# The seam between two networks: last operands in smaller steps, first copies ahead of weight casts

## The chip, the cores and the metric

One core of one Trainium2 chip. The metric is the device time of one execution in microseconds (us); before the change the median of three runs is 704.36 us. Engines are named as in the profile: PE (TensorE), DVE (VectorE), ACT (ScalarE), POOL (GpSimd), SP (SyncE, which only issues DMAs here).

## The reference, cut to what matters

```python
def _moe_ref(x, w_in, w_out):            # x: 1152 x 512, from attention; w_in 512 x 2048
    h = x @ w_in
    return np.maximum(0.01 * h, h) @ w_out            # this result is called y below

def _moe2_ref(x, domain_probs, w1, w2):  # x: y; 4 experts, w1 512 x 1024, w2 1024 x 512
    p = domain_probs / (domain_probs.sum(-1, keepdims=True) + 1e-09)
    out = 0
    for e in range(4):
        out += p[:, e:e + 1] * (np.maximum(x @ w1[e], 0.0) @ w2[e])
```

Causal attention with a decay bias (2 batches, 8 heads, 576 positions, 64 wide) comes first and gives x. The change touches the end of the first network and the start of the second.

## The kernel before, in words

All operands of matmuls are split into a rounded part and a remainder ("hi" and "lo", fp32r): a product of two tensors is three matmuls (hi by hi, lo by hi, hi by lo). ACT makes hi with a cast, DVE or POOL makes lo with a subtract.

The 1152 tokens are in two sets, set 0 of 512 and set 1 of 640. Feature-major matrices are multiplied as 2 x 2 blocks with seven block products in place of eight (`block_products`): each of the seven is 2 pairs x 3 = 6 matmuls, and four PSUM banks collect them. The order matters here: product 0 goes into bank 0; ACT copies bank 0 into `u2` (tile `tmp`); products 1, 2 and 3 go into the other banks while DVE adds up `u2` and `u4`; then three more products go *onto* banks 0, 2 and 3, which have to have been read by then. One side of a product needs prepared combinations of the four blocks of the activations (`paired_steps`, tile `t`, seven operands with hi and lo), the other side those of the weights (`seven_steps`, `seven_in_place`, `eight`, made by ACT casts and POOL).

The first network on set 1 (`mlps(phases[1])`) ends with `down1`: its results y (tile `y`, one per set, each 4 feature blocks d) are summed in SBUF by DVE, block by block in the order d = 0, 2, 1, 3, and for set 1 in two halves of 320 columns. `paired_steps(1, ...)` makes from y of set 1 the operands of the second network: first for k = 0 (feature blocks 0 and 2), then for k = 1 (blocks 1 and 3). It is a generator; the loop at its call lets it go on one step now and then between the steps of `mlps`, and empties it at the end.

The second network (`second`) runs eight blocks of half an expert each. A block has four groups of up products, here called one to four: `up_part` with pair 0 and 1 of the weights on set 0 (columns of 256: groups one and two), then pair 0 and 1 on set 1 (columns of 320: groups three and four). Groups one and two are evicted by `sevens_of`, which makes the seven operands for the down product: ACT and DVE work through the banks, four sums land in a tile `sums` of one buffer, ACT casts them, and POOL subtracts for their lo part. Then come `down2_sevens` (set 0, products of 256 columns) and `down2` (set 1, five tiles of 512 columns). Both need the two down weights of the block, each made by `eight`: a plain split (cast on ACT, subtract on POOL), four in-place combinations on POOL, and a second split. `down2` uses the plain part alone.

Weights come in by `fetch`, which `next_w` calls with a look-ahead of two pieces; raw pieces are loaded by SP into tiles `raw`. At the seam the pools of the first network (`rawp` with four raw tiles, and `ypool` with both y) are closed, and the second network's pools (`rawp2`, `wdown`) are laid over their space.

Up to the line `fixed = False` every instruction is kept in program order (class `InOrder`). After it, the order on each engine is made by the framework's scheduler, from its own model of when each instruction is ready; it places an instruction that is ready early ahead of those before it in the code. `tc.keep_in_program_order(ins)` pins one: it is queued behind the instruction that was traced last on the same engine. The subtracts of `paired_steps` are pinned so already. Each engine then takes its queue strictly in order. Since a helper records every operation, all rows show line 43; tiles tell the operations apart.

Of the kernel before, what the change touches and what calls it, by code (L numbers as in the profile page):

```python
# [9 lines left out]
F32 = mybir.dt.float32  # L10
# [9 lines left out]
def attention_moe_moe2(ctx: ExitStack, tc: tile.TileContext, q, k, v, s, w_in, w_out, probs, w1, w2, out):  # L20
# [7 lines left out]

    fixed = True

    class InOrder:

# [4 lines left out]
        def __getattr__(self, name):  # L39
            call = getattr(self.engine, name)  # L40

            def issue(*args, **kw):
                ins = call(*args, **kw)  # L43
                return tc.keep_in_program_order(ins) if fixed else ins

            return issue

# [17 lines left out]
    P = 128  # L65
    KD = DM // P
# [10 lines left out]
    sizes = (512, 2 * S - 512)  # L77

    const = ctx.enter_context(tc.tile_pool(name="const", bufs=1))
    first = ctx.enter_context(ExitStack())  # L80
    rawp = first.enter_context(tc.tile_pool(name="rawp", bufs=RAW))
    ypool = first.enter_context(tc.tile_pool(name="ypool", bufs=1))
    dram = ctx.enter_context(tc.tile_pool(name="dram", bufs=1, space=bass.MemoryType.DRAM))

    def f32(ap):
        return ap.bitcast(F32)
# [121 lines left out]
    def load_w(src, shape, unit):  # L208

        raw = rawp.tile([P, 1024], F32, tag="raw", name="raw")  # L210
        if unit is None:
            nc.sync.dma_start(raw.rearrange("p (a b) -> p a b", a=shape[0]), src)
        else:
            nc.sync.dma_start(raw, w_f32[unit])
        return raw
# [47 lines left out]
        return w  # L263

    def eight(raw):

        w = wpool.tile([P, 2, 8, 256], F32R, tag="w", name="w")
        b11, b12, b21, b22 = (raw[:, i * 256 : (i + 1) * 256] for i in range(4))

        def split(i):  # L270
            hi, lo = (w[:, l, i : i + 4].rearrange("p s c -> p (s c)") for l in range(2))
            nc.scalar.copy(hi, raw)
            nc.gpsimd.tensor_tensor(lo, raw, f32(hi), ALU.subtract)

        split(0)
        nc.gpsimd.tensor_tensor(b22, b22, b12, ALU.subtract)
        nc.gpsimd.tensor_tensor(b12, b12, b11, ALU.subtract)
        nc.gpsimd.tensor_tensor(b11, b22, b11, ALU.add)
        nc.gpsimd.tensor_tensor(b21, b21, b11, ALU.subtract)
        split(4)  # L280
        return w

    def first_sevens():

# [55 lines left out]
    stream, r64s, raws, kept, ready = [], [], {}, {}, []  # L340
# [3 lines left out]
    def fetch(n):  # L344

        if fixed:
            return
        for i in range(len(ready), min(n, len(stream))):
            if i not in raws:
                raws[i] = load_w(*stream[i][:3])  # L350
        for i in range(len(ready), min(n, len(stream))):
            ready.append(split_w(raws.pop(i), stream[i][1], stream[i][4]))

    used, w7pool = 0, None
# [26 lines left out]
    x_t, y_t, oacc, touched = [], {}, {}, {}  # L381
# [35 lines left out]
    def down1(f, c, h, w):  # L417

        if f == 0:
            y_t[c] = ypool.tile([P, KD, sizes[c]], F32, tag=f"y{c}", name=f"y{c}")  # L420
        for d in (0, 2, 1, 3):
            for lo, hi in halves(c):
                ps = ps_mm.tile([P, 512], F32, tag="mm", name="ps_d")[:, : hi - lo]
                sl, cols = slice(d * P, (d + 1) * P), slice(lo, hi)
                at_h = [at(x, cols) for x in h] if c == 0 else [at(x, j, cols) for x in h for j in range(2)]
                yield from in_steps(ps, [(at(w[i // 2], i % 2, sl), x) for i, x in enumerate(at_h)])
                ya = y_t[c][:, d, cols]
                if f == 0:
                    nc.scalar.copy(ya, ps)
                else:  # L430
                    nc.vector.tensor_tensor(ya, ps, ya, ALU.add)
                yield

    t7 = {}

    def paired_steps(s, of, pool):

        n = half[s]
        t = t7[s] = pool.tile([P, 2, 7, 2, n], F32R, tag=f"t7_{s}", name=f"t7_{s}")
        for k in range(2):  # L440
            b11, b12 = of[:, k, :n], of[:, k, n:]
            b21, b22 = of[:, 2 + k, :n], of[:, 2 + k, n:]
            sums = scratch.tile([P, 4 * 320], F32, tag="scratch", name="sums")[:, : 4 * n].rearrange("p (s t) -> p s t", s=4)
            def subtract(*args):
                tc.keep_in_program_order(nc.vector.tensor_tensor(*args, ALU.subtract))

            subtract(sums[:, 1], b12, b11)
            subtract(sums[:, 2], b22, sums[:, 1])
            yield
            subtract(sums[:, 3], b22, b12)  # L450
            subtract(sums[:, 0], b21, sums[:, 2])
            yield
            for i, j, x in ((0, 2, of[:, k::2, :n]), (2, 3, of[:, 2 + k : 3 + k, n:]), (3, 7, sums)):
                hi, lo = (t[:, l, i:j, k] for l in range(2))
                nc.scalar.copy(hi, x)
                subtract(lo, x, f32(hi))
                yield

    def paired_up(w, s, leaky):

# [45 lines left out]

    def block_products(name, n, operands):

        tmp = scratch.tile([P, 2 * 320], F32, tag="tmp", name="tmp")[:, : 2 * n].rearrange("p (i t) -> p i t", i=2)
        u2, u4 = (tmp[:, i] for i in range(2))  # L510
        bank = [ps_mm.tile([P, 512], F32, tag="mm", name=f"{name}{i}")[:, :n] for i in range(4)]

        def product(to, a, b, onto=False):
            products(bank[to], operands(a, b), onto)

        def add(to, of, x):
            nc.vector.tensor_tensor(to, of, x, ALU.add)

        product(0, 0, 0)
        nc.scalar.copy(u2, bank[0])  # L520
        product(1, 4, 5)
        add(u2, bank[1], u2)
        product(2, 3, 4)
        add(u4, bank[2], u2)
        product(3, 5, 6)
        add(bank[1], bank[3], u4)
        product(0, 1, 1, True)
        product(2, 6, 2, True)
        add(bank[2], bank[2], u2)
        product(3, 2, 3, True)  # L530
        add(bank[3], bank[3], u2)
        return bank
# [42 lines left out]

    def second(blocks):

        w, h = {}, {}

        def up_part(i, pair, s):  # L580
            if (i, pair) not in w:
                (w[i, pair],) = next_w(1)
            h.setdefault(i, ({}, {}))[pair][s] = paired_up(w[i, pair], s, False)

        for pair, s in ((0, 0), (1, 0), (0, 1), (1, 1)):
            up_part(0, pair, s)
        for i, (e, _, _) in enumerate(blocks):
            wd = next_w(2)
            down2_sevens(e, h[i], wd)
            down2(e, h.pop(i), wd)  # L590
            if i + 1 < len(blocks):
                for pair, s in ((0, 0), (1, 0), (0, 1), (1, 1)):
                    up_part(i + 1, pair, s)

    def mlps(blocks):
        hs = {}
        for what, (e, f, c), pair in in_order(blocks):
            h = hs.setdefault(f, [])
            if what == "down":
                yield from down1(f, c, h, next_w(2))  # L600
            elif c == 0 and f == 0:
                if pair == 0:
                    yield from opening(h)
            elif c == 0:
                yield from up1(next_w(1)[0], h)
            else:
                h.append(paired_up(next_w(1)[0], c, True))
                yield
# [387 lines left out]
    hpool = None  # L996
    look = 2
    t7pool = scratch = None
    last_mlp = False
    x_t.extend((None, ypool.tile([P, KD, sizes[1]], F32, tag="y1", name="x1")))  # L1000
    with ExitStack() as phase:
        x_t[0] = phase.enter_context(tc.tile_pool(name="x0pool", bufs=1)).tile([P, 2, KD, sizes[0]], F32R, name="x0")
        wpool = phase.enter_context(tc.tile_pool(name="wpool", bufs=4))
# [7 lines left out]
        with tc.tile_pool(name="early", bufs=1) as early:  # L1011
            ones = pads(early)
            sums = cumulative()
# [3 lines left out]
            for at_ in range(3 * 64):  # L1017
                i = next(side)
# [35 lines left out]
        scratch = phase.enter_context(tc.tile_pool(name="scratch", bufs=2))  # L1054
# [22 lines left out]
    with ExitStack() as phase:  # L1077
        wpool = phase.enter_context(tc.tile_pool(name="wpool", bufs=3))
        hidden_pool(phase, 3)
        scratch = phase.enter_context(tc.tile_pool(name="scratch", bufs=2))  # L1080
        tokens, rest = paired_steps(0, y_t[0], t7early), None
        last = 2 * len(phases[1]) + 32 * (len(phases[1]) - 1) + 16
        for i, _ in enumerate(mlps(phases[1])):
            if i >= 12 and i % 6 == 0:
                next(tokens, None)
            if i >= last:
                rest = rest or paired_steps(1, y_t[1], t7pool)
                if i % 4 == 1 and i < last + 16:
                    next(rest)
        for _ in tokens:  # L1090
            pass
        for _ in rest:
            pass
    first.close()
    last_mlp = True
    rawp = ctx.enter_context(tc.tile_pool(name="rawp2", bufs=2))
# [44 lines left out]
```

## Time and profile before

| | |
|---|---|
| three runs | 703.07, 704.36, 706.07 us |
| the profiled execution | 702.2 us, of which its span 700.4 |
| granted TensorE clock, mean | 0.997 of full speed |
| busy share of the span | PE 97%, PEld 89%, DVE 68%, ACT 50%, POOL 57% |
| stretch of the second network | from about 324 us to the end |

The profile is of one execution. Times in the rows count from the span's start. A timeline merges neighbouring instructions of one kind on one engine into a row: start, duration of the whole, how many; in brackets the idle time of the engine in front of it, and the engine and tile that ended it. PE is the matmul, PEld the weight load beside it. The chain of work goes back from the last instruction, at each step to what released it.

### The profile page before, as it was taken

How to read it: one execution, taken by the hardware profiler on the slowest of the kernel's cores; microseconds unless marked ns; L12 is line 12 of the kernel's file. 1: busy time of each engine (PE TensorE's matmuls, PEld its weight loads, DVE VectorE, ACT ScalarE, POOL GpSimd, SP SyncE). 2: the span in 40 equal slices, each digit the busy share in tenths (PEclk: the TensorE clock that was granted, in tenths of full speed). 3: DMA queues.
4: the chain of work that ended last, by engine and by line, in shares of the span. 5: the costliest groups of instructions: out<-in, count | busy, mean ns of one | idle time of the engine just before them, and what ended most of it. 6: DMA issues, size and time to landing. Idle time of an engine off the chain costs nothing.

```text
span 700.4 us, 12025 instructions
## 1 busy us (share of the span) xinstructions
PE 678.0 (97%) x4496; PEld 623.2 (89%) x4496; DVE 476.2 (68%) x1043; ACT 352.7 (50%) x726; POOL 401.3 (57%) x382
## 2 busy tenths in 40 slices
PE   8899999899989999998999999999999999999998
PEld 7788777778869999998999989989999899998997
DVE  6878899888798558537764747647656476465573
ACT  5768978966655765534533515415244253252520
POOL 6000213222178888952985949949679499496830
PEclk9999999999999999999999999999999999999999
DMA  8886689746632321101120110201101111112003
GB/s 225 202 221 205 189 233 269 214 138 236 225 125 79 120 91 62 61 1 61 41 53 29 61 61 6 88 30 61 61 1 61 61 34 59 31 61 61 1 31 105
DMA packets 42282, 69.15 MB, mean 99 GB/s; under 512 B 5664, under 2 KB 25904, under 8 KB 42224
## 3 DMA queue, kind: packets, MB, share of 16 engines
q1 hardware_dynamic: 32976, 40.30, 19.7%
q0 software_dynamic: 6016, 20.71, 9.5%
q10 hardware_dynamic: 3232, 7.38, 3.2%
q8 instruction: 35, 0.57, 0.4%
q14 instruction: 23, 0.19, 0.1%
HBM read 57.54 MB, written 10.82 MB: 98 GB/s over the span
## 4 chain that ended last, share of the span: by engine, by line
PE 70%; DVE 9%; issue 7%; DMA 6%; ACT 4%; POOL 4%; ACTq 0%; SPq 0%; POOLq 0%; DVEq 0%
PE ps_d L43 35%; PE ps_u L43 32%; DVE raw L43 2%; DMA r<-in_moe_w_out_dram 2%; DVE w L43 2%; PE ps_sc L43 1%; DVE z L43 1%; POOL w L43 1%; PE ps_o L43 1%; DMA vs<-in_v_dram 1%; ACT z L43 1%; PE ps_pt L43 1%; POOL raw L43 1%; DMA ke<-in_k_dram 1%; ACT w L43 1%
## 5 line engine op out<-in xcount | busy, mean ns | idle before, releaser
L43 PE MATMUL ps_u<-t,w 128*128 128x320 f32 (+1 forms) x1680 | 236.2, 299 | 3.0 <-ACT tmp L43 2.0
L43 POOL TENSOR_TENSOR w<-raw,w 128x512 fp32r<-128x512 f32 (+2 forms) x116 | 181.6, 1584 | 95.6 <-ACT w L43 95.5
L43 PEld LDWEIGHTS ps_u<-t,w 128*128 128x128 f32 x1680 | 229.9, 189 | 4.6 <-ACT tmp L43 2.4
L43 PE MATMUL ps_d<-w,ht 128*128 128x256 f32 (+1 forms) x1164 | 195.2, 326 | 0.0
L43 PEld LDWEIGHTS ps_d<-w,ht 128*128 128x128 f32 x1164 | 173.3, 190 | 18.3
L43 ACT CAST w<-raw 128x512 fp32r<-128x512 f32 (+2 forms) x138 | 98.1, 738 | 137.4 <-PE ps_d L43 88.8
L43 ACT ACTIVATE ht<-ps_u 128x320 fp32r<-128x320 f32 (+2 forms) x160 | 68.5, 436 | 93.1 <-DVE ps_u L43 67.0
L43 PE MATMUL ps_d<-ht,w 128*128 128x320 f32 (+1 forms) x576 | 108.7, 339 | 3.2 <-DVE ht L43 3.2
L43 PEld LDWEIGHTS ps_d<-ht,w 128*128 128x128 f32 x576 | 91.3, 188 | 9.6 <-DVE ht L43 3.6
L43 POOL TENSOR_TENSOR raw<-raw 128x256 f32<-128x256 f32 x120 | 86.2, 738 | 2.2
L43 DVE SCALAR_TENSOR_TENSOR oacc<-ps_d,pn,oacc 128x256 f32<-128x256 f32 (+1 forms) x92 | 51.4, 579 | 46.7 <-PE ps_d L43 46.0
L43 DVE TENSOR_TENSOR ps_u<-ps_u,tmp 128x320 f32<-128x320 f32 (+1 forms) x120 | 56.1, 470 | 34.1 <-PE ps_u L43 32.5
L43 DVE TENSOR_TENSOR tmp<-ps_u,tmp 128x320 f32<-128x320 f32 (+1 forms) x80 | 36.7, 462 | 34.6 <-PE ps_u L43 23.4
L43 DVE SCALAR_TENSOR_TENSOR ht<-ps_u,ht 128x320 fp32r<-128x320 f32 (+1 forms) x112 | 49.7, 455 | 14.3 <-ACT ht L43 14.3
L43 POOL DMA_DIRECT2D w_f<-raw x13 | 8.3, 636 | 86.8 <-DVE raw L43 73.3
L43 PE MATMUL ps_u<-x,w 128*128 128x512 f32 x192 | 56.4, 413 | 0.9 <-DVE x L43 0.9
L43 ACT ACTIVATE z<-z,mn 128x256 f32<-128x256 f32 (+4 forms) x72 | 42.5, 590 | 9.4 <-DVE mn L43 8.5
L43 DVE CUSTOM_DVE_ANT_0 z<-ps_sc,mask 128x256 f32<-128x256 f32 (+4 forms) x72 | 35.9, 499 | 10.4 <-PE ps_sc L43 6.7
L43 POOL TENSOR_TENSOR ht<-sums,ht 128x1024 fp32r<-128x1024 f32 x16 | 38.6, 2410 | 6.5 <-ACT ht L43 6.5
L43 ACT COPY pv<-ps_pt 128x512 f32<-128x512 f32 (+3 forms) x80 | 33.0, 422 | 17.8 <-PE ps_pt L43 17.5
L43 DVE TENSOR_TENSOR ht<-ps_u,ht 128x320 fp32r<-128x320 f32 (+1 forms) x48 | 26.5, 555 | 22.0 <-ACT ps_u L43 21.8
L43 PE MATMUL ps_pt<-ident,z 128*128 128x128 f32 x200 | 34.6, 276 | 6.8 <-ACT pv L43 6.0
(97 smaller groups left out, 774.1 us busy)
## 6 DMA issues: line engine op xcount, KB each, us to landing
raw<-in_moe_w_dram SPq DMA_DIRECT2D x32, 512.0 KB
raw<-w_f SPq DMA_DIRECT2D x21, 512.0 KB
w_f<-raw POOLq DMA_DIRECT2D x13, 512.0 KB, 3.5
r<-in_moe_w_out_dram POOLq DMA_DIRECT2D x6, 1024.0 KB, 7.4
r<-in_moe_w_in_dram POOLq DMA_DIRECT2D x5, 1024.0 KB, 7.6
r<-in_moe_w_in_dram ACTq DMA_DIRECT2D x3, 1024.0 KB
kd<-in_k_dram POOLq DMA_DIRECT2D x8, 288.0 KB, 8.1
kr<-in_k_dram SPq DMA_DIRECT2D x8, 288.0 KB
```

The source lines that it names most:

```text
L43: ins = call(*args, **kw)
```

## The change

`InOrder` gets a list `pinned` of engines whose instructions are pinned although `fixed` is false. It is used in three places: for DVE in the last 17 steps of the first network and the rest of `paired_steps`; for ACT's copy of bank 0 in groups one and two of the first block; for ACT in the second part of the first down weight and the whole second one.

`paired_steps` for set 1 is called with `halved`: for k = 1 its operands that are plain blocks of y are split singly as soon as their half of y is summed, and what depends on the last half comes in one step at the end. The steps at which it goes on are others.

`eight` is cut into a plain split and the rest. For the first block the look-ahead is set to nothing; the first down weight is loaded and its plain split traced before group one, its rest and the whole second weight after group two. `ypool` becomes two pools, one for each set's y.

```diff
-                return tc.keep_in_program_order(ins) if fixed else ins
+                return tc.keep_in_program_order(ins) if fixed or self.engine in pinned else ins
...
-    ypool = first.enter_context(tc.tile_pool(name="ypool", bufs=1))
+    ypools = [first.enter_context(tc.tile_pool(name=f"ypool{i}", bufs=1)) for i in range(2)]
...
     def eight(raw):
+        steps = eight_steps(raw)
+        next(steps)
+        return next(steps)
+
+    def eight_steps(raw):
...
         split(0)
+        yield
         nc.gpsimd.tensor_tensor(b22, b22, b12, ALU.subtract)
...
         split(4)
-        return w
+        yield w
...
-    def paired_steps(s, of, pool):
+    def paired_steps(s, of, pool, halved=False):
...
+            if k == 0 and halved:
+                break
+        if halved:
+            b11, b12, b21, b22 = of[:, 1, :n], of[:, 1, n:], of[:, 3, :n], of[:, 3, n:]
+            sums = scratch.tile([P, 4 * 320], F32, tag="scratch", name="sums")[:, : 4 * n].rearrange("p (s t) -> p s t", s=4)
+
+            def split(i, j, x):
+                hi, lo = (t[:, l, i:j, 1] for l in range(2))
+                nc.scalar.copy(hi, x)
+                subtract(lo, x, f32(hi))
+
+            subtract(sums[:, 1], b12, b11)
+            split(0, 1, of[:, 1:2, :n])
+            yield
+            split(1, 2, of[:, 3:4, :n])
+            yield
+            subtract(sums[:, 2], b22, sums[:, 1])
+            subtract(sums[:, 3], b22, b12)
+            subtract(sums[:, 0], b21, sums[:, 2])
+            split(2, 3, of[:, 3:4, n:])
+            split(3, 7, sums)
+            yield
...
+        was, pinned = pinned, (tc.nc.scalar,) if opening_last else pinned
         nc.scalar.copy(u2, bank[0])
+        pinned = was
...
+        look, opening_last = 0, True
+        steps = eight_steps(load_w(*stream[len(ready)][:3]))
+        next(steps)
         for pair, s in ((0, 0), (1, 0), (0, 1), (1, 1)):
             up_part(0, pair, s)
+            if (pair, s) == (1, 0):
+                pinned = (tc.nc.scalar,)
+                ready.append(next(steps))
+                fetch(used + 2)
+                look, pinned, opening_last = 2, (), False
...
         for i, _ in enumerate(mlps(phases[1])):
+            pinned = (tc.nc.vector,) if i + 1 >= last else ()
...
             if i >= last:
-                rest = rest or paired_steps(1, y_t[1], t7pool)
-                if i % 4 == 1 and i < last + 16:
+                rest = rest or paired_steps(1, y_t[1], t7pool, True)
+                if i - last in (1, 3, 5, 7, 9, 10, 13):
                     next(rest)
```

## Rows read from the trace of the kernel before

**Rows 1.** The page, part 1: busy us (share of the span), instructions.

```profile
PE 678.0 (97%) x4496; PEld 623.2 (89%) x4496; DVE 476.2 (68%) x1043; ACT 352.7 (50%) x726; POOL 401.3 (57%) x382
```

**Rows 2.** List of PE's waits: us in total, times, longest.

```profile
PE ps_u L43 <- ACT tmp L43: 2.0, 1, 2.0
...
PE ps_u L43 <- ACT sums L43: 1.0, 1, 1.0
```

**Rows 3.** Timeline of PE, 312 to 346 us: start, duration, [idle before].

```profile
323.94 5.92 PE L43 MATMUL ps_u<-t,w 128*128 128x256 f32 x48
331.84 11.20 PE L43 MATMUL ps_u<-t,w 128*128 128x256 f32 x78 [1.98 <-ACT tmp L43]
344.06 1.15 PE L43 MATMUL ps_u<-t,w 128*128 128x320 f32 x6 [1.02 <-ACT sums L43]
```

**Rows 4.** Chain of work that ended last, from 344 us: start, duration, what.

```profile
345.20 0.72 PE ps_d L43 x6
...
348.56 0.71 PE ps_d L43 x6
349.27 0.88 PE ps_u L43 x6
350.15 1.30 PE ps_d L43 x11
...
353.22 20.98 PE ps_d L43 x121
```

**Rows 5.** Timeline of ACT, 312 to 346 us.

```profile
328.26 1.26 ACT L43 CAST t<-sums 128x1280 fp32r<-128x1280 f32 x1 [2.93 <-DVE sums L43]
329.52 1.99 ACT L43 CAST w<-raw 128x1024 fp32r<-128x1024 f32 x2
331.42 0.64 ACT L43 COPY tmp<-ps_u 128x256 f32<-128x256 f32 x2
...
338.46 1.05 ACT L43 CAST ht<-sums 128x1024 fp32r<-128x1024 f32 x1 [0.27 <-DVE sums L43]
```

**Rows 6.** Timeline of DVE, 312 to 346 us.

```profile
324.14 0.49 DVE L43 TENSOR_TENSOR y<-ps_d,y 128x320 f32<-128x320 f32 x1 [0.47 <-PE ps_d L43]
...
328.14 1.22 DVE L43 TENSOR_TENSOR t<-y,t 128x640 fp32r<-128x640 f32 x2
329.56 1.49 DVE L43 TENSOR_TENSOR t<-sums,t 128x1280 fp32r<-128x1280 f32 x1 [0.19 <-ACT t L43]
331.82 1.42 DVE L43 TENSOR_TENSOR tmp<-ps_u,tmp 128x256 f32<-128x256 f32 x4 [0.77 <-ACT tmp L43]
```

**Rows 7.** Chain of work that ended last, 295 to 350 us: the weights' load.

```profile
314.87 3.90 DMA raw<-in_moe_w_dram
```

**Rows 8.** Timeline of POOL, 312 to 440 us.

```profile
330.64 5.01 POOL L43 TENSOR_TENSOR w<-raw,w 128x1024 fp32r<-128x1024 f32 x2 [13.44 <-ACT w L43]
335.62 5.62 POOL L43 TENSOR_TENSOR raw<-raw 128x256 f32<-128x256 f32 x8
...
341.19 2.40 POOL L43 TENSOR_TENSOR ht<-sums,ht 128x1024 fp32r<-128x1024 f32 x1
343.55 4.77 POOL L43 TENSOR_TENSOR w<-raw,w 128x1024 fp32r<-128x1024 f32 x2
...
374.04 4.78 POOL L43 TENSOR_TENSOR w<-raw,w 128x1024 fp32r<-128x1024 f32 x2 [8.20 <-ACT w L43]
```

**Rows 9.** DVE groups by shape, 317 to 330 us, then one of 228 to 312.

```profile
L43 DVE TENSOR_TENSOR y<-ps_d,y 128x320 f32<-128x320 f32 x8 | 3.7, 488 | 3.0 <-PE ps_d L43 2.9
...
L43 DVE TENSOR_TENSOR sums<-y 128x320 f32<-128x320 f32 x4 | 1.9, 484 | 0.0
...
L43 DVE TENSOR_TENSOR sums<-y 128x256 f32<-128x256 f32 x4 | 4.5, 1124 | 0.0
```

**Rows 10.** Timeline of ACT in the next block, 343 to 395 us.

```profile
377.86 0.37 ACT L43 COPY tmp<-ps_u 128x256 f32<-128x256 f32 x1
...
391.22 1.04 ACT L43 CAST ht<-sums 128x1024 fp32r<-128x1024 f32 x1
```

More of the change, by code (lines that the diff above doesn't have):

```diff
@@ L20, in attention_moe_moe2 @@
 def attention_moe_moe2(ctx: ExitStack, tc: tile.TileContext, q, k, v, s, w_in, w_out, probs, w1, w2, out):
-    fixed = True
+    fixed, pinned = True, ()
     class InOrder:
@@ L419, in down1 @@
         if f == 0:
-            y_t[c] = ypool.tile([P, KD, sizes[c]], F32, tag=f"y{c}", name=f"y{c}")
+            y_t[c] = ypools[c].tile([P, KD, sizes[c]], F32, tag=f"y{c}", name=f"y{c}")
         for d in (0, 2, 1, 3):
@@ L507, in block_products @@
     def block_products(name, n, operands):
+        nonlocal pinned
         tmp = scratch.tile([P, 2 * 320], F32, tag="tmp", name="tmp")[:, : 2 * n].rearrange("p (i t) -> p i t", i=2)
@@ L576, in second @@
     def second(blocks):
+        nonlocal look, pinned, opening_last
         w, h = {}, {}
@@ L998, in attention_moe_moe2 @@
     t7pool = scratch = None
-    last_mlp = False
-    x_t.extend((None, ypool.tile([P, KD, sizes[1]], F32, tag="y1", name="x1")))
+    last_mlp = opening_last = False
+    x_t.extend((None, ypools[1].tile([P, KD, sizes[1]], F32, tag="y1", name="x1")))
     with ExitStack() as phase:
@@ L1093, in attention_moe_moe2 @@
             pass
+        pinned = ()
     first.close()
```

## The prediction

> **What bounds the kernel now.** I read the page's shares first: TensorE (PE) is busy for 97% of the span [rows 1], so a gain can only come from places where it stands still. The list of PE's waits names twelve causes; ten lie in the attention or at the seams before 230 us, where the diff touches nothing. Two are late: 2.0 us on ScalarE's (ACT's) copy into tmp and 1.0 us on ACT's write of sums [rows 2]. PE's timeline puts both at the opening of the second network, at 329.86 and 343.04 us [rows 3]. That is the place of the change. It names no other after 230 us.
>
> How much the opening loses in full: its four groups of products (one and two of 256 columns, three and four of 320) are 42 matmuls each, seven products of six. The run of 48 matmuls of 256 columns took 5.92 us, 0.1233 us each [rows 3]; six of 320 columns took 0.88 us, 0.1467 each [rows 4]. So 84 x 0.1233 + 84 x 0.1467 = 22.68 us. They took from 323.94 [rows 3] to 353.22 us, less 0.72 + 0.71 + 1.30 us of down matmuls between them [rows 4]: 26.55 us. The opening loses 3.87 us, 3.0 of them in the two waits and 0.87 in small gaps. This is the most that the change can win: 0.55% of the time.
>
> Why the waits are there. PE's first group needs its copy of bank 0 (0.3 us) before it may accumulate onto that bank. ACT's order is: the cast of the last combined operands (328.26), two casts of down weights (329.52, 1.99 us together), and only then two copies, 331.42 [rows 5]; PE went on at 331.84. The first cast came late as VectorE (DVE) first ended its chain of sums, from the last sum of y at 324.14 to 329.36, the last read of y [rows 6]. The weight casts came late too: the raw weights had landed at 318.77 [rows 7], but the cast began 0.16 us after that last read of y, on whose space the new weight tile lies (all of y is in one pool); as ACT's cast before it ended at the same moment, the trace does not tell whether the space or ACT's order held it. GpSimd (POOL) stood idle for 13.44 us until 330.64 and then had both weights to do in a row: 5.01 + 5.62 us before the first group's lo part of h (341.19 to 343.59) [rows 8]. Its sums tile has one buffer, so ACT could write sums of the second group only then: that is the second wait.
>
> **The change part by part.**
> *Operands of the 640 tokens.* Two wide splits become narrow ones and move ahead; of the second half three subtracts, one narrow split and one wide split stay behind the last sum of y, in program order on DVE. One cast and one subtract more, under 0.5 us each (a pair of subtracts took 1.22 with one wide among them [rows 6]), beside PE's matmuls: DVE idles 3.0 us in front of the sums of y [rows 9]. What stays: 3 subtracts at 0.4 = 1.3 us from 324.63, a cast of 1.26 [rows 5], a subtract of 1.49 [rows 6], some 4.1 us: the chain ends at about 328.7 instead of 331.05. PE gains nothing from that alone, since the first two groups read the other operands, but DVE is free for the group's adds 2.3 us sooner.
>
> *Two pools for y, first weight early.* The first weight's tile no longer shares a pool with the y that is read last. Its first cast (1.0 us) can go out after 318.77, in ACT's gaps, and POOL's subtract (half of 5.01 = 2.5) and four combinations (half of 5.62 = 2.8) [rows 8] fall into POOL's idle time: 5.3 us less behind 330.64. That removes the cause of the second wait; its 1.02 and the 0.87 of gaps are what it can give, and the next thing late is in the next paragraph.
>
> *Copies before casts.* A pinned instruction is queued behind whatever was traced last on its engine. For the first copy that is the first weight's first cast, long done. It is then at most behind the 1.26 us cast of operands: by 325.5, or 327.5 us at the latest. Price 0 to 1.8 us: if PE is ordered to finish group one before it begins group two, it stands from 327.6 until DVE's adds behind the wide subtract (328.7 + 2 x 0.35 [rows 6] = 329.4); with the 24 matmuls of group two between, as in the 48 of [rows 3], it loses nothing. I take 0, as the trace has that order.
>
> For the second copy, the instruction traced last on ACT is the cast of group one's four sums. This is a new wait: the copy, which stood beside the first at 331.42, now comes behind all of group one's twelve DVE steps. Nine are left when the first adds are done; at 0.35 us (four took 1.42 [rows 6]) that is 3.15, plus the cast of 1.05 and the copy of 0.3 [rows 5]. With the early first copy: 328.7 + 3.15 + 1.05 + 0.3 = 333.2; with the late one about 334.7. PE has by then done 42 + 24 matmuls, to 323.94 + 66 x 0.1233 = 332.08. So it stands for 1.1 to 2.6 us, or 0 if it is ordered to begin group three (its operands end at 328.7, its banks are freed from about 331 on). Bounds 0 and 2.6. I take 1.9, the middle of the two cases without cover: nothing in the trace shows group three run ahead of group two.
>
> *Second weight later.* The remaining three weight casts are pinned behind group two's cast of sums. That cast ended 8.1 us after the copy for group one here (331.42 to 339.51 [rows 5]), and 14.4 us after it for group two of the next block (377.86 to 392.26 [rows 10]). From a copy at 333.9 that makes 342 to 348.3. Then two casts (2.0), and on POOL 2.4 for h and 2 x 2.4 [rows 8], the last of them beginning behind its cast: the second weight's plain part is there at about 349 to 355.5; before it was at 335.65 [rows 8]. PE ends the four groups at 323.94 + 22.68 + 1.9 = 348.5. Price 0.5 to 7 us, less what PE can do on the first weight alone; six matmuls of each down tile need only that. With five tiles of 512 columns this cover is 30 matmuls, so I take 0.2 us and keep both ends. POOL's own delay (some 7 us) is hidden by its idle time of 8 us or more in each later block (8.20 before 374.04 [rows 8]); without that cover the next block's first group would wait.
>
> *The sum*: -3.87 + 1.9 + 0.2 = -1.8 us (-1.77). The profiled execution took 702.2 (span 700.4 and 1.8 around it); it would be 700.4. The three runs' median, 704.36, lies 2.16 above that execution, so I subtract from the median: 702.6 us.
>
> **A row against the change.** With POOL at rest, DVE's subtracts of two tiles in SBUF took 484 ns for 320 columns (317 to 330 us); with POOL at work (228 to 312 us) they took 1124 ns for only 256 columns [rows 9]. The Trainium skill, page "SBUF — State Buffer", section "Who interferes with whom", says that such a DVE instruction and a GpSimd instruction reading SBUF share a port, and the later one is blocked for the other's whole length; these two rows agree. By that rule, and by the rows alone, moving POOL's 5.3 us under the operand chain slows the chain: the rival below.
>
> **The rivals.**
> 1. *All of it comes back*: PE runs into group three while the second copy is late, and the second weight is covered. For it: the ordering fills PE from whatever is ready, as the mixed rows [rows 4] show. Against: group three's banks come free only one by one. 704.36 - 3.87 = 700.5.
> 2. *POOL slows the operand chain*: 5.3 us of POOL work beside DVE, of which DVE's 3.0 us of idle time absorb a part: the chain and the adds behind it end 2.3 us later, and the first wait is back. For it: [rows 9]. Against: most of this work can be over by 325 us, before the part of the chain that counts. -1.77 + 2.3 = +0.5: 704.9.
> 3. *Slower: the second weight*: its casts stand in ACT's queue behind group two's last cast and PE runs dry. Place: after the fourth group, from 348.5 us. Price up to 7 us: 704.36 - 1.97 + 7 = 709.4. It decides from 2 us of standing on, and passes 0.5% at 5.5 us. For it: the 14.4 us of the next block. Against: the first weight's matmuls, and in that next block nothing hurries that cast.
> 4. *The pins change nothing on PE*: the order of PE's stream leaves the first wait as it was (1.8 of 1.98 us) and the new wait takes the second's place: -3.87 + 1.8 + 1.9 = -0.2, 704.2.
>
> **How the numbers follow.** Forecast 0.46, rival 1 0.20, rival 2 0.13, rival 3 0.14, rival 4 0.07. About 0.5%, 3.5 us, is what a measurement of this kernel can tell from no change. Faster than 700.84 is only rival 1 and the edge of the forecast: 0.17. Slower than 707.9 is the upper part of rival 3: 0.11. Same: 0.72. The range leaves out the lowest part of rival 1 and the upper part of rival 3: 700.0 to 706.6; the forecast's own is 701.2 to 704.2.
>
> **What would show it.** Right: no wait of PE on tmp at 330 us, POOL's first weight work before 326 us, one PE wait of 1 to 2.6 us before 336 us on the copy of group two, down matmuls beginning without a wait. Wrong: a wait on POOL's or ACT's weights after the fourth group (rival 3); DVE subtracts of 1 us and more at 320 to 329 us with PE waiting at 327 (rival 2); no wait at all (rival 1). A wait in a later block would mean that POOL's idle time was no cover.

## The result, and the profile after

The change made the kernel slower: 709.01 us, median of 17 runs, against 703.11 for the kernel before, 17 runs beside them. The ratio is 1.0086, 95% interval 1.006 to 1.0112. The prediction was 702.6, range 700.0 to 706.6.

One measure carries everything that follows: the **stage**, from the start of PE's first group in the second network to the start of the next block's first group. In the eleven profiles of this study it starts anywhere from 321 to 328 us. That spread arises early: from the first network's run of 96 down matmuls (230.67 us before, 234.35 after) to the stage is 93.3 us in both, and 93.3 to 93.5 in all eleven. Behind the stage, to the end of the span, every run took 326.3 to 326.5 us. Before, the stage is 374.03 - 323.94 [rows 3] = 50.1 us. These two rows are PE's timeline of the kernel before, start and duration; the second one ends the stage.

```profile
353.06 21.14 PE L43 MATMUL ps_d<-w,ht 128*128 128x256 f32 x121
374.03 18.17 PE L43 MATMUL ps_u<-t,w 128*128 128x256 f32 x138
```

After, the same timeline (the brackets are PE's waits):

```profile
327.62 5.92 PE L43 MATMUL ps_u<-t,w 128*128 128x256 f32 x48
335.66 2.68 PE L43 MATMUL ps_u<-t,w 128*128 128x256 f32 x18 [2.12 <-ACT tmp L43]
339.15 9.46 PE L43 MATMUL ps_u<-t,w 128*128 128x320 f32 x66 [0.81 <-ACT sums L43]
348.45 0.52 PE L43 MATMUL ps_d<-w,ht 128*128 128x256 f32 x3
348.81 5.44 PE L43 MATMUL ps_u<-t,w 128*128 128x320 f32 x36
354.09 3.55 PE L43 MATMUL ps_d<-w,ht 128*128 128x256 f32 x25
358.70 0.51 PE L43 MATMUL ps_d<-w,ht 128*128 128x256 f32 x2 [1.06 <-POOL w L43]
361.79 21.98 PE L43 MATMUL ps_d<-w,ht 128*128 128x256 f32 x114 [2.59 <-ACT tmp L43]
383.61 2.56 PE L43 MATMUL ps_u<-t,w 128*128 128x256 f32 x20
```

The stage is 383.61 - 327.62 = 56.0 us, 5.9 longer, as much as the medians differ. (The two profiled executions differ by 9.7; 3.7 of that lie ahead of the 96 down matmuls.) The four up groups took 354.09 - 327.62 less three down matmuls (0.36) = 26.1 us. By the same marks they took 353.06 - 323.94 less 2.73 = 26.4 before, so 0.3 us are won there. (The prediction's 26.55 goes to 353.22, the chain's mark for the same matmul [rows 4].) The **down stage**, all down matmuls with their waits, took 29.5 + 0.4 = 29.9 us against 20.97 + 2.73 = 23.7 before: 6.2 us are lost there.

The first of the old waits is still there, 2.12 us for 1.98. The second, 0.81 for 1.02 [rows 2], has the same name and another cause: PE now waits for ACT's write of *group one's* sums, ahead of group three. Group two's write, which waited for POOL before, holds PE no longer. Two new waits follow, 1.06 and 2.59.

The chain of work that ended last says how the new ones come about (start, duration, what):

```profile
350.42 1.06 ACT ht L43
...
351.55 0.92 POOL ht L43
...
353.92 2.41 POOL w L43
...
356.34 4.18 DMA raw<-in_moe_w_dram
...
360.55 0.92 ACT w L43 x2
361.47 0.28 ACT tmp L43
...
361.79 21.98 PE ps_d L43 x114
```

Read it from the end. PE waits for ACT's copy into tmp. The copy stands in ACT's queue behind a cast of the *next* block's up weight. That cast waits for a load of 4.18 us, and the load could only begin when POOL had read the first down weight for the last time and its raw buffer was free, at 356.33. POOL was that late because the casts of the down weights were pinned behind group two's cast of sums, 350.42. ACT's timeline has the same order, with the idle time in brackets:

```profile
332.34 1.26 ACT L43 CAST t<-sums 128x1280 fp32r<-128x1280 f32 x1 [0.87 <-DVE sums L43]
333.51 1.04 ACT L43 CAST w<-raw 128x1024 fp32r<-128x1024 f32 x1
335.24 0.37 ACT L43 COPY tmp<-ps_u 128x256 f32<-128x256 f32 x1 [0.69 <-DVE t L43]
...
350.42 1.05 ACT L43 CAST ht<-sums 128x1024 fp32r<-128x1024 f32 x1
351.37 1.99 ACT L43 CAST w<-raw 128x1024 fp32r<-128x1024 f32 x2
...
360.55 0.92 ACT L43 CAST w<-raw 128x512 fp32r<-128x512 f32 x2 [5.28 <-DMA raw<-in_moe_w_dram]
361.38 0.64 ACT L43 COPY tmp<-ps_d 128x256 f32<-128x256 f32 x2
```

The first three rows answer to [rows 5]: one weight cast, not two, is in front of the first copy, but the copy still starts 7.6 us after PE's first group (7.5 before), and it starts when DVE ends the operand chain, not when the cast ends.

Last, PE's stretches of 2 us (stretch, length, busy time and matmuls, granted clock):

```profile
356.00:358.00 2.00, 1.64 (x13) 1.00 0.34 25
358.00:360.00 2.00, 0.51 (x2) 1.00 0.67 236
360.00:362.00 2.00, 0.21 (x1) 1.00 0.01 2
362.00:364.00 2.00, 2.00 (x13) 0.62 0.00 0
364.00:366.00 2.00, 2.00 (x6) 0.52 0.00 0
366.00:368.00 2.00, 2.00 (x10) 1.00 0.00 0
```

From 357.64 to 361.79 PE ran two matmuls; then the granted clock fell from 1.00 (2.4 GHz) to about the half, the level of 1.2 GHz: 0.62 and 0.52 in two stretches.

### The profile page after: what moved, and what is told of

Same layout as the page of the kernel before. It is cut to its first block, busy times and chain, and to the rows that moved or that the text cites. A ratio compares the mean times of both kernels' runs of the same rounds, so it can differ in the third digit from the quotient of the medians.

```text
span 710.1 us, 12028 instructions
## 1 busy us (share of the span) xinstructions
PE 681.4 (96%) x4496; PEld 625.1 (88%) x4496; DVE 476.4 (67%) x1044; ACT 352.8 (50%) x727; POOL 400.0 (56%) x382
## 4 chain that ended last, share of the span: by engine, by line
PE 71%; DVE 11%; issue 6%; ACT 4%; DMA 4%; POOL 2%; ACTq 0%; SPq 0%; POOLq 0%; DVEq 0%
PE ps_d L43 35%; PE ps_u L43 32%; DVE raw L43 2%; DVE w L43 2%; PE ps_sc L43 2%; DVE t L43 1%; DMA r<-in_moe_w_out_dram 1%; PE ps_o L43 1%; DVE z L43 1%; DVE sums L43 1%; DVE ht L43 1%; ACT z L43 1%; PE ps_pt L43 1%; DVE y L43 1%; DMA ke<-in_k_dram 1%
## 5 line engine op out<-in xcount | busy, mean ns | idle before, releaser
L43 PE MATMUL ps_d<-w,ht 128*128 128x256 f32 (+1 forms) x1164 | 197.4, 328 | 3.7 <-ACT tmp L43 2.6
L43 PE MATMUL ps_d<-ht,w 128*128 128x320 f32 (+1 forms) x576 | 110.7, 343 | 4.2 <-DVE ht L43 4.2
```

## The experiments

All ten kernels were run beside the kernel before. The table has the stage of one profile each, and its parts: "up" is PE's time in the four up groups, "down" in the down stage, waits included. "Clock" is the lowest granted clock in a stretch of 2 us, and the part in which it fell. "Last y" and "copy" are the end of the last sum of y and the start of ACT's first copy, in us after PE's first group began.

| kernel | ratio to before (95%) | stage | up | down | clock | last y | copy |
|---|---|---|---|---|---|---|---|
| before | 1 | 50.1 | 26.4 | 23.7 | 1.00 | 0.7 | 7.5 |
| changed | 1.0086 (1.0060 to 1.0112) | 56.0 | 26.1 | 29.9 | 0.52 down | 3.4 | 7.6 |
| old opening | 1.0038 (0.9993 to 1.0083) | 53.6 | 29.9 | 23.7 | 0.50 up | 3.3 | 7.8 |
| only the opening | 1.0069 (1.0037 to 1.0102) | 54.5 | 25.4 | 29.1 | 0.50 down | 0.7 | 7.2 |
| next casts last | 1.0034 (1.0001 to 1.0068) | 52.3 | 26.1 | 26.2 | 1.00 | 3.3 | 7.6 |
| weight casts free | 1.0020 (0.9985 to 1.0055) | 50.4 | 26.7 | 23.7 | 0.50 up | 3.4 | 7.8 |
| old opening, no pin on DVE | 1.0027 (0.9984 to 1.0070) | 50.3 | 26.6 | 23.7 | 0.53 up | 0.7 | 7.6 |
| changed, sums moved, copies free | 1.0080 (1.0046 to 1.0114) | 54.1 | 23.6 | 30.4 | 0.50 down | 3.6 | 0.9 |
| before, sums moved | 0.9978 (0.9948 to 1.0008) | 47.4 | 23.7 | 23.7 | 1.00 | 0.7 | 1.3 |
| before, sums moved, two pools | 0.9978 (0.9946 to 1.0010) | 47.4 | 23.7 | 23.7 | 1.00 | 0.7 | 1.3 |
| changed, no pins, sums moved | 0.9983 (0.9952 to 1.0015) | 47.7 | 24.0 | 23.7 | 1.00 | 0.7 | 1.1 |

The ratios are uncertain by 0.3 to 0.45 per cent, some 2 to 3 us; the stage and its parts tell the variants apart where the ratio can't. But they are from one profile each, and a fall of the clock in it was worth 1.4 us where two runs allow to tell (below).

**The changed kernel with the old opening.**

```diff
-        look, opening_last = 0, True
-        steps = eight_steps(load_w(*stream[len(ready)][:3]))
-        next(steps)
         for pair, s in ((0, 0), (1, 0), (0, 1), (1, 1)):
             up_part(0, pair, s)
-            if (pair, s) == (1, 0):
...
```

> The changed kernel with the opening of the second network as it was (no early first weight, no pins on ACT); the operands' smaller steps, the pins on DVE and the two pools stay. Theory A (the loss comes from the weight casts pinned behind group two: POOL late, next block's cast in front of the down copies on ACT, and a lower clock after the standstill): no wait of PE in the first block's down stage, granted clock 1.0 there, time within 1.5 us of before. Theory B (the loss comes from the operands' chain, which ended 7.5 us after PE's first group began against 7.1 before): the whole 6 us stay, about 709.

The down stage is clean, 23.7 us with the clock at 1.00, as theory A has it. But the stage is still 53.6, 3.5 us above before and not within 1.5: theory A is not all, and theory B's whole 6 us did not stay either. The loss has moved into the up groups: a second wait on tmp of 2.85 us, in place of the 1.02 on sums, and behind it the clock at 0.71, 0.50 and 0.94. ACT's timeline of this run shows why PE waits:

```profile
341.71 1.04 ACT L43 CAST w<-raw 128x1024 fp32r<-128x1024 f32 x1 [2.15 <-POOL raw L43]
342.67 1.04 ACT L43 CAST ht<-sums 128x1024 fp32r<-128x1024 f32 x1
343.61 0.42 ACT L43 COPY tmp<-ps_u 128x320 f32<-128x320 f32 x1
```

A weight cast that waits for POOL stands ahead of group three's copy, again a head of a queue that isn't ready.

**Only the opening**: the changed kernel with the operands' steps and DVE as before.

```diff
-            pinned = (tc.nc.vector,) if i + 1 >= last else ()
...
-                rest = rest or paired_steps(1, y_t[1], t7pool, True)
-                if i - last in (1, 3, 5, 7, 9, 10, 13):
+                rest = rest or paired_steps(1, y_t[1], t7pool)
+                if i % 4 == 1 and i < last + 16:
```

> The changed kernel with the operands' steps as they were and no pins on DVE; only the opening of the second network (and the two pools) is new. Theory A: both waits of the down stage are there (some 1 us on POOL's weight, some 2.6 us on the copy behind the next block's cast), the granted clock falls behind them, and the time is 5 to 6 us above before. Theory B: about as before, within 1.5 us.

As theory A expected: waits of 1.05 on POOL's weight and 1.87 on the copy, the clock at 0.72 and 0.50 behind them, stage 54.5 (+4.4, less than the 5 to 6 expected), ratio 1.0069. The opening alone makes the kernel slower; theory B alone is refuted.

**The next block's casts behind the down copies.**

```diff
+            if i == 0:
+                look = 0
             wd = next_w(2)
             down2_sevens(e, h[i], wd)
+            if i == 0:
+                pinned = (tc.nc.scalar,)
+                fetch(used + 2)
+                look, pinned = 2, ()
```

> The changed kernel, but the next block's up weights are loaded and their casts pinned on ACT behind the first block's down copies into tmp, so that no cast that waits for a late load stands ahead of those copies. Theory A: the wait of 2.6 us on the copies goes, POOL's 1.1 us stays or grows by the few tenths that the copies took anyway, and the clock no longer falls, since the standstill is short: about 4 us below the changed kernel (705). If the second weight itself, and not ACT's queue, is the price: the standstill keeps its 3.7 us under another name and nothing is won (709).

PE's timeline of this run:

```profile
357.90 0.50 PE L43 MATMUL ps_d<-w,ht 128*128 128x256 f32 x2 [1.04 <-POOL w L43]
358.75 20.60 PE L43 MATMUL ps_d<-w,ht 128*128 128x256 f32 x114 [0.34 <-ACT tmp L43]
379.19 3.04 PE L43 MATMUL ps_u<-t,w 128*128 128x256 f32 x24
```

Its clock behind the waits (as above: stretch, length, busy time and matmuls, granted clock):

```profile
358.00:360.00 2.00, 1.66 (x12) 1.00 0.17 57
360.00:362.00 2.00, 2.00 (x11) 1.00 0.00 0
```

The 2.59 became 0.34, the granted clock stayed at 1.00, and the same 114 matmuls took 20.60 us, not 21.98. Stage 52.3: 3.65 us won, 2.25 from the wait and 1.4 from the clock. Some 1.0 on POOL stayed, as expected.

**The weight casts free**: the changed kernel without `pinned = (tc.nc.scalar,)` ahead of the rest of the first weight and the second one.

> The changed kernel without the pin on ACT for the down weights: their casts are still traced after group two, but the scheduler may place them where they are ready. Stage from PE's first group to the next block's first group: 50.1 us before, 56.0 changed. Theory A (the pins hold the second weight back): POOL has both weights some 10 us sooner, no wait of PE in the down stage, clock 1.0, stage 51 to 53.5. Rival (tracing the weights after group two is enough to make them late, pin or not): stage 56, the same two waits.

PE's timeline of this run, and its clock:

```profile
335.20 14.22 PE L43 MATMUL ps_u<-t,w 128*128 128x256 f32 x90 [2.27 <-ACT tmp L43]
...
356.27 21.26 PE L43 MATMUL ps_d<-w,ht 128*128 128x256 f32 x122
377.37 18.17 PE L43 MATMUL ps_u<-t,w 128*128 128x256 f32 x138
```

```profile
334.00:336.00 2.00, 0.80 (x3) 0.72 0.00 0
336.00:338.00 2.00, 2.00 (x11) 0.50 0.00 0
338.00:340.00 2.00, 1.90 (x13) 0.93 0.00 0
```

Stage 50.4, better than the 51 to 53.5 expected. The down stage took 23.7 us, as before, without a wait and with the clock at 1.00: the 6.2 us lost there are all gone. So the pin itself, and not the place in the code, holds the weights back; the pins on DVE and the late last sum of y are still there. PE's only wait is the first one (2.27), but behind it the clock fell, as it did not in the changed kernel. That loss is in the stage of 50.4.

**The old opening, without the pins on DVE** (`pinned = (tc.nc.vector,)` left out as well).

> As the run with the old opening (operands in smaller steps, stage 53.6 us, operand chain ending 7.8 us after PE's first group begins), but without the pins on DVE, so that the scheduler may put the sums of y first. Theory D (program order puts five other DVE steps ahead of the last sum of y, which is then 2.9 us late, and ACT's queue waits for it twice): the last sum of y comes within 1 us of PE's end, the chain ends 1 to 2 us sooner, stage 50 to 51.5. Rival (the smaller steps themselves cost it): stage 53 or more.

Stage 50.3, as before: the 3.3 us of the old-opening run come from the pins on DVE (both profiles have one fall of the clock in the up groups), and the smaller steps by themselves cost nothing that this profile shows. But theory D's mechanism fell in part: the last sum of y came 2.65 us sooner, the chain ended only 0.2 us sooner (7.3 against 7.5; the 7.8 of the expectation is the start of the copy). What differs is the order that the scheduler made for ACT: here group three's copy is ahead of the two weight casts. That the pins moved the scheduler's modelled times, and with them an order elsewhere, is my reading; no run shows the model.

**The sums tile moved.** In both kernels the program puts `tmp` of the first copy at bytes 125,792 to 128,352 of each partition, and the operands' last `sums` at 121,696 to 126,816. The edit gives the second network's `sums` a place of its own and so puts `tmp` 4,096 bytes further on, clear of them.

```diff
+    sumsp = ctx.enter_context(tc.tile_pool(name="sumsp", bufs=1))
     scratch = ctx.enter_context(tc.tile_pool(name="scratch", bufs=2))
...
-        sums = scratch.tile([P, 4 * 256], F32, tag="of_h", name="sums", bufs=1)
+        sums = sumsp.tile([P, 4 * 256], F32, tag="of_h", name="sums", bufs=1)
```

> The kernel before with one thing changed: the second network's sums tile lies in a pool of its own ahead of the scratch pool, so that the tile of the first copies (tmp) no longer lies on the space of the operands' last sums, which DVE reads to the end of the operand chain (331.05 us). Theory C (the first wait of 2.0 us comes from that space, and the order of ACT's queue followed from it): the copies go out ahead of the last cast of operands and the 2.0 us are gone; the 1.0 us on sums stays, for POOL gets the weights as late as before: about 2 us below before. Rival: ACT's weight casts hold the copies, the space does not matter: as before.

ACT's timeline of this run:

```profile
326.11 0.36 ACT L43 COPY tmp<-ps_u 128x256 f32<-128x256 f32 x1
328.62 0.37 ACT L43 COPY tmp<-ps_u 128x256 f32<-128x256 f32 x1 [2.14 <-PE ps_u L43]
329.67 1.26 ACT L43 CAST t<-sums 128x1280 fp32r<-128x1280 f32 x1 [0.68 <-DVE sums L43]
330.93 2.00 ACT L43 CAST w<-raw 128x1024 fp32r<-128x1024 f32 x2
```

The copies now stand ahead of the last cast of operands and of both weight casts, with no pin at all, and the first comes 1.3 us after PE's first group. PE waits 0.5 us in all, stage 47.4; the clock is 1.00 in this profile as in that of before. So the first wait came from the space that tmp shared; ACT's order followed from it. Expected were 2 us; the stage shows 2.7, since the wait on sums, which was to stay, went too.

**The changed kernel with the sums tile moved and the first copies free** (`opening_last` left out).

> The changed kernel with the sums tile in a pool of its own, so that tmp does not lie on the operands' last sums, and without the pins on the first copies. Theory C: the copies go out ahead of the last cast of operands and the 2.1 us wait on tmp at the start is gone; the down stage keeps its waits and its lower clock: stage 53.5 to 54.5 of 56.0. Rival (the chain on DVE holds the adds anyway): the wait only changes its name, stage 56.

The first wait is gone, the down stage keeps its waits (1.6 on POOL's weight in two parts, 1.6 on the copy) and a half clock: stage 54.1, as expected. The two losses are separate: up 23.6 us, down 30.4.

**The kernel before, sums moved and two pools for y.**

> The kernel before with the sums tile in a pool of its own (stage 47.4 us of 50.1, shown) and with the two pools for y of the change. If the space of y holds the first weight's cast, that cast goes out before the operands' last cast and POOL begins some us sooner: stage 46.5 to 47, 2.5 to 3.5 us below before. If ACT's order alone holds it (it stands behind the operands' last cast either way): stage 47.4, about 2.5 us below before.

The second case: stage 47.4 with one pool or two. The first weight cast comes 6.1 us after PE's first group either way. The space of y does not hold it; it stands behind the operands' last cast in ACT's order.

**The changed kernel without its pins, sums moved.**

> The changed kernel with none of its pins (DVE, first copies, weight casts) and the sums tile in a pool of its own; the smaller steps, the two pools and the traced order of the weights stay. If the pins and the space are all there is to it: no wait over 0.6 us, clock 1.0, stage 47 to 48 us as for the kernel before with the sums tile moved, 2 to 3 us below before. If the smaller steps or the later tracing of the weights cost something by themselves: stage 49 or more.

Stage 47.7, as expected, clock 1.00, waits of 1.1 us in all, the longest 0.90 where no more than 0.6 was expected. The stage is within 0.4 us of the kernel before with the sums tile moved: the pins and the space leave no more than that to the rest of the change.

The three kernels with the sums tile moved have the shortest stages, 2.4 to 2.7 us below before, and ratios of 0.998. Each ratio's interval includes 1: that the stage is shorter is shown in three profiles, that these kernels are faster than before as a whole is not. Against the changed kernel they are clearly faster.

## Why the prediction was wrong

- **Where it happens and the most it can win** held: nothing outside the stage moved, and moving one tile won 2.7 of the 3.87 us. Rival 3, to which I gave 0.14, was the outcome in kind and place: "its casts stand in ACT's queue behind group two's last cast and PE runs dry". That its 709.4 us is so near the measured 709.01 is luck: its price was up to 7 us of PE waiting for the second weight itself, and that wait was 1.06.
- **"Second weight later", 0.2 us**, is the term that failed most; it measured 6.2. It was taken from the cover, with no row behind it. My estimate of when the plain part is there, 349 to 355.5 us, or 25 to 31.6 after PE's first group, was right: POOL ended it at 358.65, 31.0 after, though the copy that the estimate starts from came 4.4 us later than worked out. The cover was wrong. PE's queue held 28 matmuls of 256 columns in front of the second weight's (3 and 25 in the timeline) and none of 512 columns. And I followed POOL's delay to POOL's idle time in later blocks, but not to the raw buffer that POOL frees, the load into it, and the cast at the head of ACT's queue: 2.59 of the 3.65 us of standing. The clock behind it, 1.4 us, was not in the sum; the other 1.1 us are small gaps that no run separates.
- **"The first weight's first cast, long done"** failed. The cast went out at 333.51, 5.9 us after PE's first group (5.6 before [rows 5]), and POOL stood idle for 13.75 us (13.44 before [rows 8]). A pin holds an instruction back behind another; it pulls nothing forward. So the pinned copy stood behind a late cast, and behind something later still, the next point. Why the scheduler's order has the cast behind the operands' last one although data and space were there stays open.
- **The first wait's cause** was misread, and "Copies before casts", for which I took 0, left a wait of 2.12 us. That the copy waited behind two weight casts [rows 5] was true of the queue, but the space of tmp bound it to the end of DVE's chain, and the scheduler had put the casts into that gap. The moved sums tile shows it. Rival 4, to which I gave 0.07, has nearly the up groups' sum (-0.2; measured -0.3) and the first wait left as it was, but for another reason, the order of PE's stream.
- **"The chain ends at about 328.7"**, 4.8 us after PE's first group, came out at 7.5. The part after the last sum of y was as worked out: it ended at 330.97, the chain at 335.12, 4.15 us against 4.1. But that sum was 2.7 us later than before, since program order put DVE steps ahead of it that the scheduler had put behind:

```profile
326.87 1.49 DVE L43 TENSOR_TENSOR t<-sums,t 128x1280 fp32r<-128x1280 f32 x1
328.27 0.49 DVE L43 TENSOR_TENSOR sums<-y 128x320 f32<-128x320 f32 x1
328.67 0.49 DVE L43 TENSOR_TENSOR t<-y,t 128x320 fp32r<-128x320 f32 x1
329.07 0.49 DVE L43 TENSOR_TENSOR y<-ps_d,y 128x320 f32<-128x320 f32 x1
330.08 0.49 DVE L43 TENSOR_TENSOR t<-y,t 128x320 fp32r<-128x320 f32 x1 [0.53 <-ACT t L43]
330.49 0.48 DVE L43 TENSOR_TENSOR y<-ps_d,y 128x320 f32<-128x320 f32 x1
```

  Before, the last sum of y ended 0.7 us after PE's first group had begun [rows 3, 6]; here 3.4 us.
- **The second copy's new wait, 1.9 us**, was too high: the copy came with group three's at 342.00, but PE had run ahead into group three, and 0.81 us on group one's sums is all that was left. The second wait of before did go, as forecast: group one's lo part of h ended 17.0 us after PE's first group, not 19.7 [rows 8], since POOL had only one weight to do ahead of it. The cover to which I gave only rival 1 was there.
- **Rival 2** was not put to the test: POOL was idle under the operand chain, and DVE's narrow subtracts kept their 0.48 to 0.49 us. What the Trainium skill's page "SBUF — State Buffer", section "Who interferes with whom", says of a DVE instruction with two SBUF inputs beside a GpSimd instruction that reads SBUF agrees with [rows 9], but no run here shows it at this place. Those two rows are means and show the direction; one subtract behind the mean of 1124 ns took 2.31 us (266.18 to 268.49) beside a subtract of POOL's (265.80 to 268.22).

In sum the up groups gave 0.3 us, not 1.97, and the down stage took 6.2, not 0.2.

## What to carry to other kernels

A pin in a queue taken strictly in order is a wait for everything behind it, so follow each pinned instruction's *consumers* as far as the buffers that they free, the loads into these, and whatever else waits for the load. Where an instruction waits longer than its data explain, look first at what lay on its tile's space: here moving one tile undid a wait that two sets of pins had left in place. And measure a stage by two marks in the trace when runs differ by more than the change is worth, and read the granted clock inside it before two stages are compared.

## What the runs showed of the hardware

The granted clock's price was unexpected. After PE had stood from 357.64 to 361.79 us but for two matmuls, the clock was 0.62 and 0.52 in the next two stretches of 2 us, and the same 114 matmuls took 1.4 us longer than in the run where PE stood for 1.04 and 0.34 us and the clock stayed at 1.00. A fall also stands behind single, shorter standstills, but not behind each. In the run with the old opening and no pin on DVE, PE stood once, for 2.11 us, and the clock fell:

```profile
328.98 13.46 PE L43 MATMUL ps_u<-t,w 128*128 128x256 f32 x84 [2.11 <-ACT tmp L43]
```

```profile
330.00:332.00 2.00, 2.00 (x13) 0.61 0.00 0
332.00:334.00 2.00, 2.00 (x12) 0.53 0.00 0
```

The 2.27 us of the run with free weight casts lowered it too. The 2.12 us in front of 335.66 in the changed kernel's trace did not:

```profile
336.00:338.00 2.00, 1.99 (x17) 1.00 0.00 0
```

Nor did 2.27 us in front of 332.89 with the old opening, or 2.12 with the next casts last. What decides between these is not shown here. So that the clock stayed at 1.00 in one profile is no promise for other executions, and stages that differ by less than 1.5 us are told apart only by their waits.
